# Attention into a mixture of experts on one core: batch 0's routing at earlier steps, casts dealt to other engines, weight loads placed otherwise

## The chip, the cores and the metric

One core of a Trainium2 chip runs the whole program. Times are device microseconds (us) of one execution. PE is TensorE, DVE is VectorE, ACT is ScalarE, POOL is GpSimd, and SP is the engine that only issues DMAs here.

## The reference, cut to what matters

There are three parts, one after the other. First comes attention over 2 batches of 8 heads with 768 rows and head size 64, in which a row sees only the keys of its own hash bucket. Its output, 1536 tokens of 512 numbers, goes through a layer of 8 experts, and that through a dense layer.

```
mask   = q_bucket[:, :, :, None] == k_bucket[:, :, None, :]
scores = np.where(mask, scale * q @ k.T, -1e9);  attn = softmax(scores);  x = attn @ v
expert_idx = argmax(x @ w_gate);  gate = softmax(x @ w_gate)[expert_idx]
disp[e, count[e]] = x[i]                     # tokens in order, up to capacity
out[i] = gate[i] * relu(disp[e] @ w1[e]) @ w2[e]
g = h * clip(h + 3, 0, 6) / 6  with  h = out @ w_in;   result = g @ w_out
```

To find a token's place, the kernel needs the expert of every token before it. This is the routing. It can be done for batch 0 once batch 0's heads are through, and for batch 1 only after the last head.

## The kernel before, in words

Products that need float32 precision are made from two f16 halves each: a high half (a cast) and a low half (the difference, scaled). So every weight, probability and activation is split into `h` and `l` tiles.

**Attention** is a loop over 96 steps `k`, six for each of 16 heads. In step `k` PE makes the scores of one tile of 128 keys (L442, L443), ACT takes the exponential into `pf` (L444), `high` casts it to `phi` (ACT L452, or DVE L454), `low` two steps later makes `plo` (L458, POOL or DVE), and four or five steps later `pv` multiplies both by v (L470 to L472). The row maxima of `mx` (PE L425, DVE L428) run eight steps ahead. All other work is put into the loop by the tables of `Q`: `at(k, f)` calls `f` at step `k`, and `spread(k, gen, d)` runs a generator piece by piece every `d` steps. Within an engine the instructions run in the order in which they are emitted.

In the last 12 steps, 84 to 95, `Q["hl"]` lists the steps (less 84) whose `high` is DVE's, the others being ACT's, and `Q["ll"]` those whose `low` is POOL's, the others being DVE's. In the middle of the loop nearly every `low` is POOL's.

`route(b, ...)` (L207) is the routing of one batch in 20 pieces: maximum (L212), difference `dl` (L215), rank `sc`, one-hot `oh`, counts, the PE product `psr`, positions, and at the end six one-hots `ohr` of 128x128 (L263). `weigh(b)` (L267) makes the gate weights in seven pieces, up to `rg` (L203).

**Between attention and the experts** lie, in order: the last `pv`; `scaled` and `columns` (L480 to L488) on DVE; six ACT copies into `xp` (L845); `store(7)` of these rows to `xd` in DRAM (SP, L512); batch 1's routing on DVE; the products `windows` into `psw`, from which the token numbers `ids` come (L1096); `gather(0)` (POOL, L970), which reads the first expert's tokens from `xd`; then `gates` (L1103), `scale_x` (L978), and `make_x` (PE transposes L989, ACT `xh` L992, DVE `xl` L993) for the two tiles of 112 tokens; then the first product of expert 0, `gemm1` (L1006). `heat` (L1083) adds products that nothing reads.

**Weights.** `load_w(e, i, q)` loads 512 KB into one of six `raw` buffers (SP, L143). `high_w` casts on ACT (L157), `low_w` makes the low halves on DVE (L163) for all that `high_w` has listed, and `split_w` does both for 512 columns. Before the change the four tiles of w1 of expert 0 are loaded in steps 78 to 81, w1's first half is split in steps 88.5 to 94.5, its second half around the gather, and the four tiles of w2 are loaded behind `store(7)`, for SP issues them as soon as that store is issued.

From the first `gemm1` on, experts and dense layer follow without a gap on PE; the output rows are written at the end.

Of the kernel before, what the change touches and what calls it, by code (L numbers as in the profile page):

```python
# [9 lines left out]
F32 = mybir.dt.float32  # L10
# [11 lines left out]
NH = B * H  # L22
BITS = 6
NC = S // P
# [39 lines left out]
def moe_attention_kernel(ctx, tc, qk, v, vt, pj, wg, w1, w2, win, wout, out, cap):  # L64
    nc = tc.nc
    pe, act, dve, pool, sp = nc.tensor, nc.scalar, nc.vector, nc.gpsimd, nc.sync
# [16 lines left out]
    def persist(shape, dt, name):  # L83
        return const.tile(shape, dt, tag=name, name=name)

    xd = dram.tile([NT + 1, DM], F32, tag="xd", name="xd")
    ident = persist([P, P], F32, "ident")
    ones = persist([P, P], F32, "ones")
    upper = persist([P, P], F16, "upper")
# [47 lines left out]
    wp1 = opened(wctx, "wp1", 2, side="right")  # L137
# [11 lines left out]
    late = []  # L149
# [7 lines left out]
        act.activation(wh[e, i][:, c : c + n], r, AF.Copy, scale=(S1, S2)[i // 2])  # L157
        late.append((e, i, c, n, r))

    def low_w():  # L160
        while late:
            e, i, c, n, r = late.pop(0)
            dve.scalar_tensor_tensor(  # L163
                out=wl[e, i][:, c : c + n], in0=r, scalar=(S1, S2)[i // 2], in1=wh[e, i][:, c : c + n],
                op0=ALU.mult, op1=ALU.subtract, accum_out=wlo[:, nlo[0] : nlo[0] + 1],
            )
            nlo[0] += 1

    def split_w(wp, e, i, q):
        high_w(wp, e, i, 512 * q, 512)  # L170
        low_w()
# [35 lines left out]
    def route(b, psum):  # L207

        n = NC
        l3 = lg[:, b]  # L210
        t1 = rtile([n], f"mx{b}")
        dve.tensor_reduce(out=t1, in_=l3, axis=AX.X, op=ALU.max)  # L212
        yield
        dl = dl_t[b] = rtile([n, E], f"dl{b}")
        dve.tensor_tensor(out=dl, in0=l3, in1=bc(t1, E), op=ALU.subtract)  # L215
        yield
        sc = rtile([n, E], f"sc{b}")
        dve.scalar_tensor_tensor(out=sc, in0=dl, scalar=0.0, in1=mid(rank8, n), op0=ALU.is_ge, op1=ALU.mult)
        yield
        dve.tensor_reduce(out=t1, in_=sc, axis=AX.X, op=ALU.max)  # L220
        yield
        o = oh[:, b]
        dve.tensor_tensor(out=o, in0=sc, in1=bc(t1, E), op=ALU.is_equal)
        yield
        with nc.allow_low_precision("counts up to 6"):
            dve.tensor_reduce(out=rs[:, b], in_=o.rearrange("p c e -> p e c"), axis=AX.X, op=ALU.add)
        yield
        ps = psum()
        k3 = ps[:, 0 : n * E].rearrange("p (c e) -> p c e", e=E)
        for c in range(n - 1):  # L230
            pe.matmul(k3[:, c + 1 :], ident16, mid(o[:, c], n - 1 - c), start=c == 0, stop=False, skip_group_check=True)
        for i in range(b):
            pe.matmul(k3, ones16, mid(rs[:, i], n), start=False, stop=False, skip_group_check=True)
        pe.matmul(k3, upper, mid(rs[:, b], n), start=False, stop=True, skip_group_check=True)
        yield
        dve.tensor_tensor(out=sc, in0=k3, in1=o, op=ALU.mult)
        yield
        dve.tensor_reduce(out=pos[:, b], in_=sc, axis=AX.X, op=ALU.add)
        yield
        ge = rtile([n, NW + 1], f"ge{b}")  # L240
        dve.tensor_tensor(out=ge, in0=bc(pos[:, b], NW + 1), in1=mid(edges, n), op=ALU.is_ge)
        yield
        dve.tensor_reduce(out=t1, in_=ge[:, :, 1:NW], axis=AX.X, op=ALU.add)
        dve.tensor_tensor(out=jo[:, b], in0=ge[:, :, 0:NW], in1=ge[:, :, 1 : NW + 1], op=ALU.subtract)
        yield
        place = rtile([n], f"pl{b}")
        dve.scalar_tensor_tensor(out=place, in0=t1, scalar=-float(GW), in1=pos[:, b], op0=ALU.mult, op1=ALU.add)
        jt = rtile([n, NW], f"jt{b}")
        dve.scalar_tensor_tensor(
            out=jt, in0=bc(tokid[:, b * n : (b + 1) * n], NW), scalar=1.0, in1=jo[:, b], op0=ALU.add, op1=ALU.mult  # L250
        )
        yield
        spots(rh[:, b], o, jt, pool if b else dve)
        yield
        for c in range(n):
            if not b:
                yield
            if b and c == n - 1:
                off = rtile([P], "off")
                act.activation(off, iota_r, AF.Square, bias=place[:, c : c + 1], scale=-1.0)  # L260
                act.activation(ohr[:, b, c], off, AF.Relu, bias=1.0, scale=-1.0)
                continue
            dve.tensor_scalar(  # L263
                out=ohr[:, b, c], in0=iota_r, scalar1=place[:, c : c + 1], scalar2=None, op0=ALU.is_equal
            )

    def weigh(b):  # L267

        n = NC
        ex = rtile([n, E], f"ex{b}")  # L270
        act.activation(ex, dl_t[b], AF.Exp, scale=isw[:, 0:1])
        yield
        se = rtile([n], f"se{b}")
        dve.tensor_reduce(out=se, in_=ex, axis=AX.X, op=ALU.add)
        yield
        dve.tensor_scalar(out=se, in0=se, scalar1=EPS, scalar2=None, op0=ALU.add)
        yield
        dve.reciprocal(out=gt[:, b], in_=se)
        yield

        jt = rtile([n, NW], f"jg{b}")
        dve.tensor_tensor(out=jt, in0=jo[:, b], in1=bc(gt[:, b], NW), op=ALU.mult)
        j2 = rtile([n, 2 * NW], f"j2{b}", F16)
        dve.tensor_copy(j2[:, :, 0:NW], jt)
        yield
        dve.tensor_tensor(out=jt, in0=jt, in1=j2[:, :, 0:NW], op=ALU.subtract)
        dve.tensor_scalar(out=j2[:, :, NW:], in0=jt, scalar1=LS, scalar2=None, op0=ALU.mult)
        yield
        spots(rg[:, b], oh[:, b], j2)
# [8 lines left out]
                )  # L298


    Q = {'v': (-3.25, -4.75, -1.75, -2.25), 'vg': (-4.5, -4.75), 'vgd': 1, 'pr': (-13.0, -12.75, -12.0, -12.5), 'prd': 0.6, 'b0': 7.75, 'b': 1.75, 'bd': 0.5, 'vm0': (8.0, 8.25, 10.75, 13.0), 'vm': (-0.5, 4.75, 7.0, 12.25), 'vs': 13.25, 'pa': 1.5, 'ev': 0.5, 'lvt': -5.0, 'v4': (2.0, 3.75, 4.0, 16.25), 'vg0': (1.85, -4.4, 7.75), 'p2': 3.5, 'lr': (0, 3, 1.5, 4.5), 'lv': 5.5, 'vsd': 0.75, 'ac': (0, 0, 2, 6, 7, 8, 9, 10), 'hd': (3, 5, 17), 'hn': (4, 4, 2, 2, 4, 3, 0, 0, 0), 'ap': (0,), 'h0': (7,), 'hl': (4,), 'l0': (), 'll': (1, 10), 'ht': (5, 9)}


    with ExitStack() as actx:
# [38 lines left out]
        def misc(name):  # L343
            return ps_x.tile([P, 512], F32, tag="x", name=name)
# [412 lines left out]
        def at(k, f, *args):  # L757
            later.setdefault(k, []).append((f, args))

        def spread(k, gen, d=1):  # L760


            def part(k):
                if next(gen, gen) is not gen:
                    at(k + d, part, k + d)

            at(k, part, k)
# [18 lines left out]
        for h in range(NH):  # L786
# [8 lines left out]
            elif h < NH - 1:  # L795
                at(k + Q["pa"], pair, h // 2)
                at(NC * h + Q["lvt"], load_vt, h // 2 + 1)
        spread(66, route(0, lambda: misc("psr0")), 1.5)
        spread(84, weigh(0))
        spread(89, any_unmatched())  # L800
        for i in range(4):
            at(NC * (NH - 3) + i, load_w, 0, i // 2, i % 2)
            at(STEPS - 7.5 + 2 * i, split_w, wp1, 0, 0, i)

        def due(k):
            for q in sorted(q for q in later if q <= k):
# [3 lines left out]
        for k in range(STEPS + LAG + 2):  # L810
# [17 lines left out]
                    pv(u)  # L828
            due(k)
        assert not later  # L830
        tally(NH // 2 - 1, pool, (0,))
        ru = nc.values_load(nflag[0:1, NH // 2 : NH // 2 + 1], min_val=0, max_val=NH * S)
        with tc.If(ru > 0):
# [11 lines left out]
            act.activation(xp_t[h // 2][:, c, DE : DE + D], sums[0][:, c, 0:D], AF.Copy, scale=sums[1][:, c])  # L845
        store(h // 2)
        rgen = route(1, lambda: misc("psr2"))
        for _ in range(8):
            next(rgen)
        heat(ps_t, "t", 2)  # L850


# [129 lines left out]
    def make_x(e, j):  # L982
        if j == 0:
            xs_t[e] = tuple(xp.tile([P, KD, W], F16, tag=n, name=f"{n}{e}") for n in ("xh", "xl"))
        xh, xl = xs_t[e]
        t = xg_t.pop((e, j))
        ps = ps_a.tile([P, KD, P], F32, tag="a", name=f"psa{e}{j}")
        for k in range(KD):
            pe.transpose(ps[:, k], t[:, k * P : (k + 1) * P], ident)  # L989
        c = slice(j * GW, (j + 1) * GW)  # L990
        ps = ps[:, :, 0:GW]
        act.activation(xh[:, :, c], ps, AF.Copy, scale=SX)  # L992
        dve.scalar_tensor_tensor(out=xl[:, :, c], in0=ps, scalar=SX, in1=xh[:, :, c], op0=ALU.mult, op1=ALU.subtract)  # L993
# [96 lines left out]
    windows(ps1, ohr, rh, range(B - 1))  # L1090
    wgen = weigh(1)
    next(wgen)
    windows(ps2, ohr, rg, range(B - 1))
    run(rgen)
    windows(ps1, ohr, rh, [B - 1])
# [8 lines left out]
    dve.scalar_tensor_tensor(  # L1104
        out=gates, in0=ps2[:, :, NW:], scalar=1.0 / LS, in1=gates, op0=ALU.mult, op1=ALU.add
    )
    split_w(wp1, 0, 1, 0)
    split_w(wp1, 0, 1, 1)
    for j in range(2):
        scale_x(0, j)  # L1110
    for j in range(2):
        make_x(0, j)
    for q in range(2, 4):
        split_w(wp1, 0, 1, q)
    for q in range(4):
        load_w(0, 2 + q // 2, q % 2)
    tgen = totals(lambda: ps_a.tile([P, KD * P], F32, tag="a", name="psc"))
    cgen = compact(lambda: ps_a.tile([P, KD * P], F32, tag="a", name="psi"))

# [354 lines left out]
```

## Time and profile before

| what | us |
|---|---|
| median of 3 runs (range) | 677.04 (676.58 to 677.83) |
| the profiled execution's own time | 675.88 |
| its span, first to last instruction | 674.1 |
| PE busy in it | 638.4 (95%) |
| DVE busy | 481.0 (71%) |
| ACT busy | 426.6 (63%) |
| POOL busy | 229.8 (34%) |

The mean granted clock of PE over the span is 0.981 of full speed. Read the shares by stage: attention lies in 0 to 238 us, the stretch between attention and experts in 238 to 255 us, the experts in 255 to 411 us, and the dense layer after that. In a chain of waits each line is the piece of work that the next line waited for, so the chain ends with the program. In a timeline the bracket behind an instruction is the time its engine stood idle before it, and who ended that.

### The profile page before, as it was taken

The page shows a single profiled execution, that of the slowest core. Times are in us where ns is not written, and L with a number is a line of the kernel's source. Part 1 is how long each engine was busy: PE and PEld are TensorE (multiplying, and loading weights), DVE is VectorE, ACT ScalarE, POOL GpSimd, SP SyncE. Part 2 cuts the span into 40 slices and gives each one's busy share as a digit, 9 for nine tenths or more (in the row PEclk, how much of TensorE's full clock was granted, in tenths as well). Part 3 has the DMA queues.
Part 4 walks back from the last instruction along what each step waited for, and adds up shares of the span by engine and source line. Part 5 has one row for each costly group of instructions (what it writes and reads, how often), then busy time and mean ns, then how long its engine had stood idle before and what let it go on. Part 6 is the DMA issues. An engine that isn't in the chain of part 4 may idle for free.

```text
span 674.1 us, 14367 instructions
## 1 busy us (share of the span) xinstructions
PE 638.4 (95%) x5518; PEld 479.7 (71%) x5518; DVE 481.0 (71%) x1038; ACT 426.6 (63%) x869; POOL 229.8 (34%) x199
## 2 busy tenths in 40 slices
PE   7899999999999769999999999999999999999894
PEld 2588889989899638999999997555555555555541
DVE  6768898898999957888888877888888452222320
ACT  3467778778787826776667765455445576555730
POOL 4339769769778233221077500000000021000011
PEclk9889999999999978999999999999999999999998
DMA  8584764764465065777677735443442011000011
GB/s 236 127 233 115 231 177 122 233 169 109 126 160 165 25 217 193 250 246 257 213 253 228 243 115 162 137 145 126 150 134 92 0 48 48 1 0 1 1 41 59
DMA packets 37840, 94.14 MB, mean 140 GB/s; under 512 B 7576, under 2 KB 13720, under 8 KB 37760
## 3 DMA queue, kind: packets, MB, share of 16 engines
q1 hardware_dynamic: 34672, 85.71, 42.7%
q0 software_dynamic: 2400, 7.36, 3.2%
q8 instruction: 46, 0.75, 0.4%
q14 instruction: 34, 0.28, 0.1%
q10 hardware_dynamic: 688, 0.03, 0.1%
HBM read 67.14 MB, written 6.29 MB: 109 GB/s over the span
## 4 chain that ended last, share of the span: by engine, by line
PE 75%; DVE 10%; DMA 6%; ACT 5%; issue 2%; SPq 0%; POOL 0%; POOLq 0%; ACTq 0%; DVEq 0%
PE psg L1249 16%; PE pso L1276 15%; PE psh L1006 11%; PE psy L1033 11%; PE psm L425 5%; PE pst L442 4%; PE pst L443 3%; DVE mx L428 2%; DMA out_dram<-os,inv 2%; PE psv L470 2%; PE psv L471 2%; PE psv L472 2%; PE psg L531 2%; DMA vr<-in_v_dram 1%; ACT junk L1203 1%
## 5 line engine op out<-in xcount | busy, mean ns | idle before, releaser
L458 POOL TENSOR_TENSOR plo<-pf,phi 128x768 f16<-128x768 f32 x86 | 147.1, 1736 | 60.4 <-ACT phi L452 24.9
L444 ACT ACTIVATE pf<-pst 128x384 f32<-128x384 f32 x192 | 83.5, 486 | 47.4 <-PE pst L443 45.7
L428 DVE TENSOR_REDUCE mx<-psm 128x1 f32<-128x384 f32 x192 | 96.3, 548 | 20.0 <-PE psm L425 19.7
L1291 POOL DMA_INDIRECT out_dram<-os,inv x12 | 12.1, 1008 | 270.8 <-DVE os L1283 244.5
L163 DVE SCALAR_TENSOR_TENSOR wl<-raw,wh 128x1024 f16<-128x1024 f32 (+1 forms) x68 | 82.7, 1218 | 6.3 <-ACT wh L157 5.2
L1249 PE MATMUL psg<-yTh,ch 128*128 128x512 f16 (+1 forms) x256 | 83.4, 326 | 3.2 <-DVE rl L1252 3.2
L1249 PE MATMUL psg<-yTl,ch 128*128 128x512 f16 (+1 forms) x256 | 83.4, 326 | 0.0
L1249 PE MATMUL psg<-yTh,cl 128*128 128x512 f16 (+1 forms) x256 | 83.4, 326 | 0.0
L1252 DVE SCALAR_TENSOR_TENSOR rl<-rl,psg 128x512 f32<-128x512 f32 x64 | 35.0, 551 | 64.4 <-ACT rl L1251 64.0
L442 PE MATMUL pst<-Y,K 128*128 128x384 f32 x192 | 75.2, 392 | 2.0 <-ACT pf L444 2.0
L1249 PEld LDWEIGHTS <-ch 128*128 128x128 f16 x512 | 50.0, 98 | 35.9
L452 ACT ACTIVATE phi<-pf 128x768 f16<-128x768 f32 x85 | 71.7, 844 | 1.9
L1276 PE MATMUL pso<-ch,gh 128*128 128x512 f16 x192 | 72.8, 379 | 0.0
L1276 PE MATMUL pso<-ch,gl 128*128 128x512 f16 x192 | 72.8, 379 | 0.0
L1276 PE MATMUL pso<-cl,gh 128*128 128x512 f16 x192 | 72.8, 379 | 0.0
L425 PE MATMUL psm<-K,X 76*128 76x384 f32 x192 | 66.8, 431 | 4.6 <-DVE mx L428 3.8
L157 ACT ACTIVATE wh<-raw 128x1024 f16<-128x1024 f32 (+1 forms) x68 | 67.6, 999 | 0.5 <-issue 0.4
L1276 PEld LDWEIGHTS <-gh 128*128 128x128 f16 x384 | 37.6, 98 | 42.3
L443 PE MATMUL pst<-X,K 77*128 77x384 f32 x192 | 66.5, 346 | 0.0
L1033 PE MATMUL psy<-hh,wl 128*128 128x224 f16 x256 | 66.3, 259 | 0.0
L1033 PE MATMUL psy<-hh,wh 128*128 128x224 f16 x256 | 66.3, 259 | 0.0
L1033 PE MATMUL psy<-hl,wh 128*128 128x224 f16 x256 | 66.3, 259 | 0.0
(231 smaller groups left out, 1495.2 us busy)
## 6 DMA issues: line engine op xcount, KB each, us to landing
raw<-in_w_dram SPq DMA_DIRECT2D x64, 512.0 KB
rc<-in_win_dram SPq DMA_DIRECT2D x16, 512.0 KB
rc<-in_wout_dram SPq DMA_DIRECT2D x16, 512.0 KB
r<-in_qk_dram SPq DMA_DIRECT2D x16, 384.0 KB
K<-hi SPq DMA_DIRECT2D x31, 192.0 KB
vr<-in_v_dram SPq DMA_DIRECT2D x4, 768.0 KB
vt<-in_vt_dram SPq DMA_DIRECT2D x8, 384.0 KB
Y<-hi SPq DMA_DIRECT2D x16, 192.0 KB
```

The lines of the kernel that those rows point to most:

```text
L163: dve.scalar_tensor_tensor(out=wl[e, i][:, c : c + n], in0=r, scalar=(S1, S2)[i // 2], in1=wh[e, i][:, c : c + n], op0=ALU.mult, op1=ALU.s ...
L425: pe.matmul(ps[:, :HS], st["X"][0:76, c::NC], st["K2"][0:76, n * HS : (n + 1) * HS], start=True, stop=True)
L428: dve.tensor_reduce(out=mm[:, c, n : n + 1], in_=ps[:, :HS], axis=AX.X, op=ALU.max)
L442: pe.matmul(ps[:, :HS], st["K1"][:, kc], st["Y"][:, qc], start=True, stop=False)
L443: pe.matmul(ps[:, :HS], st["K2"][0:77, kc], st["X"][0:77, qc], start=False, stop=True)
L444: act.activation(pf.rearrange("k (c n p) -> k c n p", c=NC, n=2)[:, :, n], ps[:, :HS].rearrange("k (p c) -> k c p", c=NC), AF.Exp, scale=0 ...
L452: act.activation(phi_t[k], pf_t[k], AF.Copy)
L458: eng.tensor_tensor(out=plo_t[k], in0=pf_t.pop(k), in1=phi_t[k], op=ALU.subtract)
L1006: pe.matmul(ps, l[:, c], r[:, k], start=n == 0, stop=n == 3 * KD - 1)
L1033: pe.matmul(ps, l, r, start=n == 0, stop=n == 3 * KF - 1)
L1249: pe.matmul(ps, l, x, start=n == 0, stop=n == 3 * KD - 1)
L1276: pe.matmul(po[blk][s], l, r, start=first and n == 0, stop=last and n == 2)
```

## The change

- Batch 0's `route` begins at step 57 instead of 66, and its `weigh` at step 75 instead of 84.
- Of the last 12 steps' `high`, DVE takes steps 88, 90, 92 and 94 instead of 88 alone. The `low` of step 94 goes from POOL to DVE.
- In the loop only two of the four splits of w1's first half are left whole (88.5 and 91), the third is cast at step 93; the remaining casts of `high_w` stand behind the loop and in batch 1's routing, and their `low_w` are put one by one into places in which DVE waits.
- w1's loads move from steps 78 to 81 to steps 81.5 to 84.5, the loads of w2's first half from behind `store(7)` to steps 88 and 89. The loads of w2's second half stand behind a DMA of one number, `held`, that reads the gathered tile `xg` after `scale_x`, so SP waits there.
- `make_x` of tile 0 is emitted ahead of `scale_x` of tile 1. Idle products: 5 before the gates and 6 (was 9) behind them, and new ones, 3 behind `make_x` of tile 0 and 2 behind that of tile 1.

```diff
+    held = dram.tile([1, 1], F32, tag="held", name="held")
...
-    def low_w():
-        while late:
+    def low_w(most=99):
+        for _ in range(min(most, len(late))):
...
-    Q = { ... 'hl': (4,), 'l0': (), 'll': (1, 10), 'ht': (5, 9)}
+    Q = { ... 'hl': (4, 6, 8, 10), 'l0': (), 'll': (1,), 'ht': (5, 6, 3, 2)}
...
-        spread(66, route(0, lambda: misc("psr0")), 1.5)
-        spread(84, weigh(0))
+        spread(57, route(0, lambda: misc("psr0")), 1.5)
+        spread(75, weigh(0))
         spread(89, any_unmatched())
         for i in range(4):
-            at(NC * (NH - 3) + i, load_w, 0, i // 2, i % 2)
-            at(STEPS - 7.5 + 2 * i, split_w, wp1, 0, 0, i)
+            at(STEPS - 14.5 + i, load_w, 0, i // 2, i % 2)
+        for i in range(2):
+            at(STEPS - 8 + i, load_w, 0, 2, i)
+            at(STEPS - 7.5 + 2.5 * i, split_w, wp1, 0, 0, i)
+        at(STEPS - 3, high_w, wp1, 0, 0, 1024, 512)
...
         assert not later
+        high_w(wp1, 0, 0, 1536, 512)
+        for q in range(2):
+            high_w(wp1, 0, 1, 512 * q, 512)
+        low_w(1)
         tally(NH // 2 - 1, pool, (0,))
...
         rgen = route(1, lambda: misc("psr2"))
-        for _ in range(8):
+        for _ in range(7):
             next(rgen)
+        low_w(1)
+        next(rgen)
         heat(ps_t, "t", 2)
...
     next(wgen)
+    high_w(wp1, 0, 1, 1024, 512)
     windows(ps2, ohr, rg, range(B - 1))
...
-    split_w(wp1, 0, 1, 0)
-    split_w(wp1, 0, 1, 1)
-    for j in range(2):
-        scale_x(0, j)
-    for j in range(2):
-        make_x(0, j)
-    for q in range(2, 4):
-        split_w(wp1, 0, 1, q)
-    for q in range(4):
-        load_w(0, 2 + q // 2, q % 2)
+    high_w(wp1, 0, 1, 1536, 512)
+    low_w(1)
+    scale_x(0, 0)
+    low_w(1)
+    make_x(0, 0)
+    heat(HT[2])
+    scale_x(0, 1)
+    make_x(0, 1)
+    heat(HT[3])
+    sp.dma_start(out=held, in_=xg_t[0, 1][0:1, 0:1])
+    for q in range(2):
+        load_w(0, 3, q)
```

## Rows read from the trace of the kernel before

**Rows 1.** The chain that ended last, whole run: start us, us, what.
```profile
247.42 5.70 DMA xg<-xd,ids
...
255.04 2.02 PE psh L1006 x12
...
257.09 9.00 PE psh L1006 x84
...
276.25 9.20 PE psh L1006 x96
```

**Rows 2.** DVE by line, 219 to 236 us: count, busy us, mean ns, idle before.
```profile
L458 DVE TENSOR_TENSOR plo<-pf,phi 128x768 f16<-128x768 f32 x8 | 7.6, 948 | 0.0
...
L263 DVE TENSOR_SCALAR ohr<-iota_r,pl 128x128 f16<-128x128 f16 x6 | 2.8, 473 | 0.0
...
L163 DVE SCALAR_TENSOR_TENSOR wl<-raw,wh 128x512 f16<-128x512 f32 x4 | 2.7, 682 | 0.1
...
L203 DVE TENSOR_TENSOR rg<-oh,j 128x384 f16<-128x384 f16 x1 | 0.6, 552 | 0.0
...
L454 DVE CAST phi<-pf 128x768 f16<-128x768 f32 x1 | 0.6, 551 | 0.0
```

**Rows 3.** DVE in order of time: start, us, line, operation, idle before and its releaser.
```profile
177.84 1.03 DVE L215 TENSOR_TENSOR dl<-lg,mx 128x48 f32<-128x48 f32 x1
...
233.60 1.63 DVE L263 TENSOR_SCALAR ohr<-iota_r,pl 128x128 f16<-128x128 f16 x1
...
238.13 0.22 DVE L480 TENSOR_SCALAR rd<-psv,sc 128x6 f32<-128x6 f32 x1 [1.09 <-PE psv L472]
...
239.41 0.21 DVE L215 TENSOR_TENSOR dl<-lg,mx 128x48 f32<-128x48 f32 x1
...
241.34 0.21 DVE L236 TENSOR_TENSOR sc<-psr,oh 128x48 f32<-128x48 f32 x1 [0.73 <-PE psr L234]
...
243.99 0.19 DVE L1096 CAST ids<-psw 128x32 int32<-128x32 f32 x1 [0.33 <-PE psw L295]
...
246.96 0.19 DVE L1104 SCALAR_TENSOR_TENSOR gates<-psg,gates 128x32 f32<-128x32 f32 x1
...
250.79 0.55 DVE L978 TENSOR_SCALAR xg<-xg,gates 128x512 f32<-128x512 f32 x1 [2.42 <-issue]
...
253.54 0.62 DVE L993 SCALAR_TENSOR_TENSOR xl<-psa,xh 128x448 f16<-128x448 f32 x1
```

**Rows 4.** ACT in order of time, same columns.
```profile
233.85 0.84 ACT L452 ACTIVATE phi<-pf 128x768 f16<-128x768 f32 x1
...
238.92 1.33 ACT L845 ACTIVATE xp<-psv,rd 128x64 f32<-128x64 f32 x6 [4.23 <-DVE xp L488]
```

**Rows 5.** POOL in order of time, same columns.
```profile
233.13 2.04 POOL L458 TENSOR_TENSOR plo<-pf,phi 128x768 f16<-128x768 f32 x1 [11.71 <-PE psv L472]
...
245.81 1.31 POOL L970 DMA_INDIRECT xg<-xd,ids  x1 [2.69 <-DMA raw<-in_w_dram]
```

**Rows 6.** The gathers' line L970, 16 of them: issue to landing.
```profile
DMA to landing us min/median/max: 3.9/5.2/7.2
```

**Rows 7.** SP's queue in order of time: store 6 and store 7 issued.
```profile
220.43 0.55 SPq L512 DMA_DIRECT2D xd<-xp  x1
...
240.28 0.54 SPq L512 DMA_DIRECT2D xd<-xp  x1
```

**Rows 8.** GB/s of 219 to 226 us in 40 slices (0.175 us each).
```profile
GB/s 0 0 0 0 0 0 0 17 1 0 0 0 0 0 0 196 331 295 316 307 304 313 182 3 0 0 0 0 0 0 0 0 0 0 0 0 0 0 0 0
```

**Rows 9.** PE by line, 238 to 255 us, columns as Rows 2.
```profile
L989 PE MATMUL psa<-ident,xg 128*128 128x128 f32 x8 | 1.3, 283 | 3.5 <-DVE xg L978 3.5
```

**Rows 10.** One microsecond: length, busy us (PE, PEld, DVE, ACT, POOL), PEclk, DMA share, GB/s.
```profile
255.00:256.00 1.00, 0.96 (x8) 0.85 (x8) 0.98 (x2) 1.00 (x3) 0.93 (x2) 0.73 0.00 0
```

**Rows 11.** Columns as Rows 10, from the row maxima of heads 7 and 11 to the next.
```profile
116.08:128.44 12.36, 12.05 (x152) 10.97 (x149) 10.93 (x28) 10.27 (x20) 7.89 (x8) 1.00 0.72 184
...
168.05:180.78 12.73, 12.29 (x150) 10.96 (x148) 11.75 (x31) 10.71 (x21) 7.98 (x7) 1.00 0.68 174
```

More of the change, by code (lines that the diff above doesn't have):

```diff
@@ L298, in windows @@
                 )
-    Q = {'v': (-3.25, -4.75, -1.75, -2.25), 'vg': (-4.5, -4.75), 'vgd': 1, 'pr': (-13.0, -12.75, -12.0, -12.5), 'prd': 0.6, 'b0': 7.75, 'b': 1.75, 'bd': 0.5, 'vm0': (8.0, 8.25, 10.75, 13.0), 'vm': (-0.5, 4.75, 7.0, 12.25), 'vs': 13.25, 'pa': 1.5, 'ev': 0.5, 'lvt': -5.0, 'v4': (2.0, 3.75, 4.0, 16.25), 'vg0': (1.85, -4.4, 7.75), 'p2': 3.5, 'lr': (0, 3, 1.5, 4.5), 'lv': 5.5, 'vsd': 0.75, 'ac': (0, 0, 2, 6, 7, 8, 9, 10), 'hd': (3, 5, 17), 'hn': (4, 4, 2, 2, 4, 3, 0, 0, 0), 'ap': (0,), 'h0': (7,), 'hl': (4,), 'l0': (), 'll': (1, 10), 'ht': (5, 9)}
+    Q = {'v': (-3.25, -4.75, -1.75, -2.25), 'vg': (-4.5, -4.75), 'vgd': 1, 'pr': (-13.0, -12.75, -12.0, -12.5), 'prd': 0.6, 'b0': 7.75, 'b': 1.75, 'bd': 0.5, 'vm0': (8.0, 8.25, 10.75, 13.0), 'vm': (-0.5, 4.75, 7.0, 12.25), 'vs': 13.25, 'pa': 1.5, 'ev': 0.5, 'lvt': -5.0, 'v4': (2.0, 3.75, 4.0, 16.25), 'vg0': (1.85, -4.4, 7.75), 'p2': 3.5, 'lr': (0, 3, 1.5, 4.5), 'lv': 5.5, 'vsd': 0.75, 'ac': (0, 0, 2, 6, 7, 8, 9, 10), 'hd': (3, 5, 17), 'hn': (4, 4, 2, 2, 4, 3, 0, 0, 0), 'ap': (0,), 'h0': (7,), 'hl': (4, 6, 8, 10), 'l0': (), 'll': (1,), 'ht': (5, 6, 3, 2)}
     with ExitStack() as actx:
@@ L985, in make_x @@
         xh, xl = xs_t[e]
-        t = xg_t.pop((e, j))
+        t = xg_t[e, j]
         ps = ps_a.tile([P, KD, P], F32, tag="a", name=f"psa{e}{j}")
```

## The prediction

> **What bounds the kernel now.** I read the chain of waits first, because it says where a change can reach the end. From 276 us on it is PE alone: 96 products of an expert take 9.20 us without a gap [rows 1], and the next expert begins where the last one ends. So whatever the change does up to the first product of expert 0 (255.04 us) moves the end one for one, and nothing behind it is touched unless weights come late. Second, DVE by line for 219 to 236 us, the last steps of attention [rows 2], and DVE, ACT and POOL in order of time [rows 3 to 5]. The reader is to see that DVE's last `low` ends at 237.04 (238.13 less the 1.09 of waiting), while ACT's last cast ended at 234.69 (233.85 + 0.84): DVE ends attention there. Third, the stretch 238 to 255 us: a serial chain of small DVE pieces, a store, a gather, and a first expert that starts at half clock.
>
> The sum is made against the profiled execution: 675.88 us, of which 674.1 is the span and 1.8 lies around it. The median of the three runs is 1.16 above it; I add that at the end.
>
> **Part 1, DVE in the last steps.** What leaves DVE behind 219 us: six `ohr` (2.8 us in all), two of the four `wl` (2 x 0.68 = 1.35), `rg` (0.55) [rows 2], and five small pieces of `weigh`, which I put at 0.2 each like the unhindered `dl` (0.21) of [rows 3]: together 5.7. What comes: three casts of 0.55 and one `plo` of 0.95 [rows 2], together 2.6. The net is 3.1 less. Neighbouring durations overlap at their ends, which favours the longer list, so I take 2.8, and 0.2 for PE, which no longer has several steps' products waiting when the last `low` comes: 3.0. ACT loses three casts of 0.84 [rows 4] and one weight cast, so it moves forward as far and DVE stays the last. Bounds: 0.5, if ACT or PE takes over, and 3.8. The two `wl` return at no cost: one stands behind the last `low`, where DVE waited 1.09, one in the wait for `psr` of 0.73 [rows 3], and each is 0.68 and an accumulator read. Without that cover they would cost 1.35. The three weight casts behind the loop stand on ACT, which was idle for 4.23 us ahead of the `xp` copies [rows 4].
>
> **Part 2, batch 0's routing earlier.** The pieces that leave the end go to steps 75 to 85, where POOL makes the `low`. There a DVE piece is not what it is alone: `dl` takes 1.03 us beside POOL against 0.21 without it, and the `ohr` of 233.60 takes 1.63 [rows 3], while POOL's `plo` runs from 233.13 to 235.17 [rows 5]; the other five take (2.8 - 1.63) / 5 = 0.24. So a piece can wait until POOL's instruction ends. POOL is busy 7.98 of 12.73 us in such a stretch [rows 11], so a piece meets it with a chance of 0.63 and waits half of 2.04: 0.64 us on average. Moved are six `ohr` at 0.24, `rg` and five small ones, 3.0 us, and they make some eight such meetings (pieces emitted together count once), 5.1 us: DVE gets 8.1 us more before step 87. What that does to the time is read from [rows 11]: between heads 11 and 12, where the maximum and `dl` of batch 0 lay, DVE was busy 0.82 longer than a period earlier, and the stretch was 0.37 longer, a share of 0.45. I take 0.45 x 8.1 = 3.6 us later. Bounds: nothing, as DVE has idle time there (0.98 us of 12.73), and all 8.1. The earlier pieces of `route` (steps 57 to 75 instead of 66 to 84) leave one busy stretch for another and cancel.
>
> The Trainium skill has a rule for this ("SBUF — State Buffer", section "Who interferes with whom"): a DVE instruction with two SBUF inputs, or one in a mode that uses both ports, and a POOL instruction that reads SBUF exclude each other, and the second one blocks fully. The trace agrees in `dl` and in `ohr`. By that rule alone every one of the moved pieces could wait out a whole POOL instruction, and attention would get longer by more than I take; that case is the slower rival below.
>
> **Part 3, store, gather, first tiles.** Store 6 was alone on the queues: issued at 220.43 [rows 7], its bytes move in slices 15 to 22 (counted from 0), until 223.0 [rows 8], 2.6 us after issue. Store 7 was issued at 240.28 with four loads of 512 KB straight behind it. The gather waited for 2.69 us until 245.81 for a DMA [rows 5], though the token numbers were there at 244.18 [rows 3]. The page names a weight load; the gather can only need the store. In the changed kernel nothing follows the store, so it lands near 243.0, and the token numbers are last: the gather starts at 244.25, 1.55 earlier. Its flight was 4.98 (245.81 to the scaling at 250.79 [rows 3]) beside the loads; without them I take 4.1, near the shortest of all gathers, 3.9 [rows 6]. So tile 0 is there at 248.35. The gates are ready at 247.15 [rows 3], the `wl` put behind them ends near 247.9, still under cover. From the landing of tile 1 (247.42 + 5.70 = 253.12) to the first product (255.04) it took 1.92 us [rows 1]; tile 0 needs that and 0.62 for its `xl` [rows 3], so DVE comes to tile 1 at 250.9, after its landing near 250.0, and the first product follows 1.92 later, at 252.8: 2.2 earlier. Bounds: 0.6, if the flight stays at 5.2 and only the start moves, less what the order on DVE costs, and 2.9.
>
> The added wait on SP holds back only the two loads of w2's second half and what follows them. They go out near 252 and are first needed by ACT half-way through the first `gemm1`, 4.6 us after its start (half of 9.20 [rows 1]), near 257.4; two loads of 512 KB at the 300 GB/s of the store [rows 8] take 3.5 us. I take nothing.
>
> **Part 4, the clock.** The first 96 products took 2.02 + 9.00 us against 9.20 later [rows 1]: 1.8 us lost, since the granted clock fell from 2.4 to 1.2 GHz in 255 to 256 (mean 0.73 [rows 10]), after PE had stood idle 3.5 us in two waits for `xg` [rows 9]. Earlier tiles and five idle products between them leave, by the times of part 3, about 1.3 us of idle. I take the whole 1.8; the other end is 0.
>
> **Sum:** +3.6 - 3.0 - 2.2 - 1.8 = -3.4 us, 672.5 for a profiled execution, 673.6 for the median.
>
> **Rivals.** (a) The waits for POOL are absorbed: PE and DVE have gaps, and the pieces fall into them. For it speaks POOL's 4.75 us idle in 12.73 [rows 11], against it that DVE is busy 11.75 of it. Then part 2 is 0: 670.0. (b) The clock still falls, as 1.3 us of idle remain: 675.4. (c) The tail is not DVE's: with shorter DVE work ACT's exponentials, or PE, set the pace, part 1 is worth 0.5: 676.1. Against it, ACT ended 2.35 us ahead of DVE and is relieved as well. (d) The weights behind the held DMA come some 2 us late, and ACT, which runs in order, keeps the first products waiting: 675.6. (e) Slower: the moved `ohr` and gate pieces wait for POOL and every wait reaches the end. At 1.39 for each of six `ohr` (1.63 - 0.24) and 0.82 for two others (1.03 - 0.21) that is 3.0 + 8.3 + 1.6 = 12.9 instead of 3.6: 682.9. It decides from 8.4 on, where it eats the 7.0 of the other parts and 1.35 more, that is, if all 8.1 pass and a little more. For it speaks that DVE is the busiest of the engines that could wait; against it the share of 0.45.
>
> **How the numbers follow.** About 0.2% (1.35 us) is what a measurement can tell from no change here: faster is under 675.69, slower over 678.39. Forecast 0.56, by itself 671.3 to 676.0 (0.51 faster, 0.05 same); (a) 0.13, faster; (b) 0.10 (0.06 faster, 0.04 same); (c) 0.07 (0.02, 0.05 same); (d) 0.05 (0.02, 0.03 same); (e) 0.09, slower. That is 0.74 faster, 0.17 same, 0.09 slower. The range 669.6 to 677.6 takes in (a) to (d) and leaves out (e) and the outer ends of the parts.
>
> **What would show it.** Part 1: DVE's wait before the first `rd` after the last `pv` shrinks to that of one step's products, and attention from the last row maximum to there takes about 3 us less. Part 2: the last row maximum (218.9 before) comes 3 to 4 us later, and `ohr` instructions of over 1 us stand in steps 78 to 85. Part 3: the gather begins within 0.2 us of the token numbers, and its flight is near 4. Part 4: the first 96 products take 9.2 to 9.4, with no granted clock under 1 after 249. The prediction fails if the last maximum moves by over 8 us or not at all, or if the gather still waits for a DMA.

## The result: slower by 1.2%, lost in the steps of attention that got batch 0's routing

The changed kernel takes 684.71 us (median; 683.97 to 685.02) against 676.81 of the kernel before in the same comparison: ratio 1.0116, 95% interval 1.0087 to 1.0144. Forecast were 673.6, with 677.6 as the upper end. The profiled execution of the changed kernel took 685.02 us, its span is 683.3 (before 675.88 and 674.1).

Where the time went can be read at five marks that both traces have: head 10's and head 15's last row maximum, the first `rd` behind the last `pv`, the first product of expert 0, and that of expert 1.

| stretch | before | after | difference |
|---|---|---|---|
| start to head 10's last maximum | 154.96 | 156.32 | +1.36 |
| heads 10 to 15 (steps 57 to 87) | 63.94 | 76.49 | +12.55 |
| last maximum to the last `rd` | 19.23 | 17.69 | -1.54 |
| `rd` to the first product of expert 0 | 16.91 | 14.77 | -2.14 |
| expert 0 | 21.21 | 19.77 | -1.44 |
| sum: start of expert 1 | 276.25 | 285.04 | +8.79 |

The rest of the 9.2 us of span, 0.4, lies in the output writes. The first line is not the change's: it arises before head 3's maximum (65.53 against 64.16), where both programs are the same, behind a stretch of half clock at 54 to 58 us. Two executions of one and the same kernel, `e1_old_steps` and `e11_old_steps_again` below, have head 3's maximum at 65.89 and at 64.14.

So three of the four parts brought something, and part 2 cost more than all of them. First the three stretches that hold 11.45 of its 12.55, in the kernel before (length; busy us of PE, PEld, DVE, ACT, POOL with counts; granted clock; DMA share; GB/s):

```profile
180.78:194.66 13.88, 13.61 (x177) 12.66 (x174) 13.21 (x29) 10.44 (x20) 13.04 (x8) 1.00 0.32 76
194.66:206.11 11.45, 11.07 (x137) 10.09 (x136) 10.32 (x22) 9.86 (x18) 7.93 (x8) 1.00 0.89 238
206.11:218.90 12.79, 12.79 (x163) 12.00 (x160) 11.90 (x30) 9.94 (x20) 10.40 (x7) 1.00 0.41 134
```

and the same steps in the changed kernel:

```profile
183.24:199.75 16.51, 14.39 (x166) 13.08 (x163) 14.94 (x31) 11.31 (x22) 14.64 (x9) 0.95 0.39 101
199.75:216.31 16.56, 12.98 (x141) 11.88 (x139) 15.87 (x30) 10.00 (x18) 10.22 (x8) 0.81 0.40 102
216.31:232.81 16.50, 16.50 (x162) 15.67 (x160) 11.91 (x29) 9.95 (x19) 6.81 (x5) 0.73 0.36 129
```

The middle row shows DVE busy for 15.87 of 16.56 us with one instruction fewer than in the row above it. The last row shows something else: there DVE is busy for no longer than before (11.91), and PE, at a mean granted clock of 0.73, is busy without a gap. DVE in order of time, the changed kernel:

```profile
188.41 1.62 DVE L242 TENSOR_TENSOR ge<-pos,edges 128x30 f32<-128x30 f32 x1
...
195.15 1.62 DVE L248 SCALAR_TENSOR_TENSOR pl<-mx,pos 128x6 f32<-128x6 f32 x1
...
204.15 1.29 DVE L277 TENSOR_SCALAR se<-se 128x6 f32<-128x6 f32 x1
...
209.34 1.01 DVE L283 TENSOR_TENSOR jg<-jo,gt 128x24 f32<-128x24 f32 x1
210.39 1.56 DVE L285 CAST j<-jg 128x24 f16<-128x24 f32 x1
211.86 1.70 DVE L264 TENSOR_SCALAR ohr<-iota_r,pl 128x128 f16<-128x128 f16 x1
```

In the kernel before, `jg` and its cast had no `low` of POOL beside them (DVE in order of time):

```profile
221.19 0.27 DVE L282 TENSOR_TENSOR jg<-jo,gt 128x24 f32<-128x24 f32 x1
221.49 0.18 DVE L284 CAST j<-jg 128x24 f16<-128x24 f32 x1
```

POOL in order of time, the changed kernel (the first row is three instructions of 1.6 each, and the second begins with the third of them):

```profile
208.66 4.84 POOL L459 TENSOR_TENSOR plo<-pf,phi 128x768 f16<-128x768 f32 x3 [1.63 <-PE pst L444]
211.86 3.23 POOL L459 TENSOR_TENSOR plo<-pf,phi 128x768 f16<-128x768 f32 x2
```

`jg` ends at 210.35, its cast at 211.95, `ohr` at 213.56: each at the end of one POOL instruction. 24 numbers per partition take 1.0 and 1.6 us instead of 0.27 and 0.18. I read it so: between two pieces that DVE issues back to back POOL starts its next `low`, and the second piece waits for all of it; `e6_pool_halves` below tests that. PE then waits for the row maxima behind this pile (PE in order of time, the same kernel):

```profile
214.07 0.70 PE L426 MATMUL psm<-K,X 76*128 76x384 f32 x1 [3.58 <-DVE mx L429]
```

and its granted clock falls while it stands (one microsecond each, columns as in Rows 10):

```profile
211.00:212.00 1.00, 0.00 (x0) 0.00 (x0) 1.00 (x2) 0.97 (x2) 1.00 (x2) 0.82 0.38 105
212.00:213.00 1.00, 0.00 (x0) 0.00 (x0) 1.00 (x1) 0.09 (x1) 1.00 (x1) 0.50 0.01 3
...
225.00:226.00 1.00, 1.00 (x16) 1.00 (x15) 0.42 (x2) 0.00 (x0) 1.00 (x1) 0.85 0.44 176
```

It is at 1.2 GHz from 211.7 to 225.3, and there PE is the engine without idle time, while DVE waits for its products. A shorter stretch of this kind lies at 198 to 201.

What answers to [rows 3] to [rows 5] behind attention, DVE in order of time and POOL in order of time:

```profile
250.50 0.22 DVE L481 TENSOR_SCALAR rd<-psv,sc 128x6 f32<-128x6 f32 x1 [0.34 <-PE psv L473]
...
256.14 0.19 DVE L1107 CAST ids<-psw 128x32 int32<-128x32 f32 x1 [0.33 <-PE psw L296]
...
261.04 0.48 DVE L988 TENSOR_SCALAR xg<-xg,gates 128x512 f32<-128x512 f32 x1 [1.11 <-issue]
```

```profile
257.30 1.08 POOL L980 DMA_INDIRECT xg<-xd,ids  x1 [2.02 <-DVE j L285]
```

The weight load that [rows 5] named is gone from the gather's wait, and tile 0 is scaled 3.74 us after the gather's issue instead of 4.98. The store that the gather reads from, SP's queue in order of time, and GB/s of 252 to 259 us in 40 slices (its last bytes move near 255.9):

```profile
252.64 0.56 SPq L513 DMA_DIRECT2D xd<-xp  x1
```

```profile
GB/s 0 0 0 0 0 0 0 0 94 0 70 310 328 322 316 322 310 179 23 20 23 20 3 0 0 0 0 0 0 0 0 0 0 0 0 0 0 0 0 0
```

What answers to [rows 1], from the chain that ended last, and to [rows 10]:

```profile
265.27 1.31 PE psh L1016 x12
...
285.04 9.20 PE psh L1016 x96
```

```profile
265.00:266.00 1.00, 0.80 (x9) 0.73 (x8) 0.75 (x2) 1.00 (x2) 0.65 (x1) 1.00 0.63 106
```

Expert 0 begins at full clock.

### The profile page after: what moved, and what is told of

Same layout as the page of the kernel before. It is cut to its first block, busy times and chain, and to the rows that moved or that the text cites. A ratio compares the mean times of both kernels' runs of the same rounds, so it can differ in the third digit from the quotient of the medians.

```text
span 683.3 us, 14368 instructions
## 1 busy us (share of the span) xinstructions
PE 644.5 (94%) x5520; PEld 485.1 (71%) x5520; DVE 488.0 (71%) x1042; ACT 424.9 (62%) x866; POOL 225.6 (33%) x198
## 4 chain that ended last, share of the span: by engine, by line
PE 53%; ACT 3%; DMA 3%; DVE 2%; issue 1%; POOL 0%; POOLq 0%; DVEq 0%
PE psg L1262 16%; PE pso L1289 15%; PE psy L1043 11%; PE psh L1016 10%; DMA out_dram<-os,inv 2%; ACT junk L1216 1%; PE psa L999 1%; ACT gh L1272 1%; DVE rl L1265 1%; DVE wl L164 0%; ACT rl L1264 0%; DMA xg<-xd,ids 0%; ACT xh L1002 0%; DVE hl L1020 0%; DVE xg L988 0%
## 5 line engine op out<-in xcount | busy, mean ns | idle before, releaser
L459 POOL TENSOR_TENSOR plo<-pf,phi 128x768 f16<-128x768 f32 x85 | 143.8, 1715 | 60.2 <-ACT phi L453 30.5
L426 PE MATMUL psm<-K,X 76*128 76x384 f32 x192 | 68.6, 437 | 11.9 <-DVE mx L429 10.3
L453 ACT ACTIVATE phi<-pf 128x768 f16<-128x768 f32 x82 | 69.2, 843 | 1.9
L426 PEld LDWEIGHTS psm<-K,X 76*128 76x128 f32 x192 | 53.8, 313 | 20.7 <-DVE mx L429 16.3
L471 PE MATMUL psv<-vh,phi 128*128 128x73 f16 x576 | 67.5, 202 | 0.0
L473 PE MATMUL psv<-vh,plo 128*128 128x73 f16 x576 | 66.8, 200 | 0.5 <-DVE plo L459 0.4
```

The source lines that it names most:

```text
L426: pe.matmul(ps[:, :HS], st["X"][0:76, c::NC], st["K2"][0:76, n * HS : (n + 1) * HS], start=True, stop=True)
L453: act.activation(phi_t[k], pf_t[k], AF.Copy)
L459: eng.tensor_tensor(out=plo_t[k], in0=pf_t.pop(k), in1=phi_t[k], op=ALU.subtract)
```

## The experiments

"Stretch" is the one from head 10's last row maximum to head 15's: 63.94 us before, 76.49 in the changed kernel. Stretches are from one trace each. Ratios are to the kernel before, taken beside it, with 95% intervals. Beside `e1_old_steps` to `e4_gather_alone` the kernel before took 680.82 us, 4 more than above, so their medians are to be read against that. Some traces hold a wait of the kind told under "not expected" in unchanged steps, worth 4.6 us in `e1_old_steps` and 5.7 in `e2_steps_alone`; so the stretch tells more than the median.

**The steps undone, and the steps alone.** `e1_old_steps` is the changed kernel with

```
-        spread(57, route(0, lambda: misc("psr0")), 1.5)
-        spread(75, weigh(0))
+        spread(66, route(0, lambda: misc("psr0")), 1.5)
+        spread(84, weigh(0))
```

> The changed kernel with batch 0's route and weigh back at steps 66 and 84, all else changed. Theory P (the moved pieces meet POOL's low instructions, DVE is held, PE waits for row maxima and its clock falls): the last row maximum, 232.8 us in the changed kernel, comes back to 219 to 221, no half clock in attention, and the time is 672 to 676. Rival Q (the routing's steps are harmless; the weight loads bunched at steps 81.5 to 84.5 and the casts given to DVE delay attention): the last maximum stays near 232 and the time at 683 to 686.

`e2_steps_alone` is the kernel before with the opposite edit and nothing else.

> The kernel before with only batch 0's route and weigh moved to steps 57 and 75. P: the last row maximum moves from 218.9 to about 231, the clock is at half in parts of 195 to 230, DVE's end of attention gets shorter by 2 to 4, and the time is 683 to 689, slower than before. Q: the last maximum within 1.5 us of before and the time 674 to 677.

Measured: ratio 0.9938 (0.9885 to 0.9991) for the first (679.08 us), 1.0184 (1.0080 to 1.0289) for the second (694.32). The last maxima, at 225.56 and 239.22, missed the expected times, as both traces lose over 6 us before head 10. The windows of the stretch, first of `e1_old_steps`, then of `e2_steps_alone`:

```profile
161.55:225.56 64.01, 62.59 (x770) 57.58 (x768) 58.34 (x137) 51.87 (x98) 52.29 (x35) 1.00 0.52 138
```

```profile
161.58:239.22 77.64, 71.13 (x772) 65.25 (x768) 66.51 (x149) 52.70 (x98) 51.77 (x35) 0.87 0.43 114
```

The steps alone bring the whole loss, and without them the moved loads and shared casts add nothing to the stretch. The rival with the loads and casts is out. The second kernel's tail from the last maximum to `rd` is 18.00, the first one's 19.00, before 19.23; 2 to 4 us less were expected of the second.

**One piece elsewhere.** `e3_onehots_on_act` is the changed kernel with batch 0's one-hots on ACT:

```
-            if b and c == n - 1:
+            if not b or c == n - 1:
```

> The changed kernel with the six one-hots ohr of batch 0 made on ACT (Square, then Relu, as batch 1's last one is), at the same steps. P: the three ohr that took 0.73, 1.70 and 1.37 us leave DVE, the other waits (sc, ge, place, the add, jg and its cast) stay; the pile of jg, cast and ohr at 209 to 213.5 gets shorter by its last 1.7, so part of the loss goes: 677 to 682. Q: no change, 683 to 686.

Measured: 1.0117 (1.0067 to 1.0167), 685.82 us, stretch 74.12. The expected time was missed: the three long `ohr` are gone, but the next pieces meet POOL in their place (the last two of `weigh` before `rg` take 0.76 and 1.56 us there, 0.73 and 0.18 in the changed kernel), and the clock falls at 211 all the same. Taking away these pieces was not enough while others made the same pile.

`e5_weigh_late` is the changed kernel with the gate weights alone at their old step:

```
-        spread(75, weigh(0))
+        spread(84, weigh(0))
```

> The changed kernel with weigh back at step 84 and route still at 57. The stretch from head 10's to head 15's last row maximum is 63.9 us in the kernel before and 76.5 in the changed one. Theory P (every moved piece waits out POOL's instruction, DVE falls behind, PE waits and its clock falls): the add, jg, its cast and the difference (1.29, 1.01, 1.56, 0.73 us) leave, so the pile at 209 to 213.5 is gone, PE's wait of 3.6 us shrinks and the clock holds at least after 212: stretch 68 to 72. If route's pieces alone do the harm (ge 1.62, place 1.62, ohr 1.70): 74 to 77.

Measured: 1.0033 (0.9998 to 1.0068), stretch 67.77 with DVE busy 61.25 and a mean clock of 0.97 (half clock at 192 to 195 alone). So `weigh` beside `route` makes 8.7 of the 12.55, and `route`'s own new steps 3.8.

**Shorter POOL instructions.** `e6_pool_halves` is the changed kernel with

```
+            x, n = pf_t.pop(k), S // 2 if eng is pool and k > 53 else S
+            for c in range(0, S, n):
+                eng.tensor_tensor(out=plo_t[k][:, c : c + n], in0=x[:, c : c + n], in1=phi_t[k][:, c : c + n], ...)
```

> The changed kernel with POOL's low from step 54 on made by two instructions of 384 columns instead of one of 768. If a DVE piece waits until the POOL instruction in flight ends and then has its turn, the waits halve to under 0.9 us each, PE's long wait goes and the clock holds: stretch of heads 10 to 15 at 65 to 70 us instead of 76.5, time near before or up to 4 us under it. If POOL's next instruction can go ahead of a waiting DVE piece, waits of 1.5 us and more stay and the stretch stays at 73 to 78.

Measured: 1.0088 (1.0055 to 1.0120), 682.82 us, and in its profile the stretch is 68.79. Window of the stretch, and two lines of DVE by line in it:

```profile
156.98:225.77 68.79, 63.84 (x770) 58.03 (x767) 62.75 (x148) 52.25 (x98) 57.65 (x65) 1.00 0.48 129
```

```profile
L219 DVE SCALAR_TENSOR_TENSOR sc<-dl,rank 128x48 f32<-128x48 f32 x1 | 0.9, 922 | 0.0
...
L285 DVE CAST j<-jg 128x24 f16<-128x24 f32 x1 | 0.8, 837 | 0.0
```

`sc` took 1.66 and this cast 1.56 in the changed kernel. Half the POOL instruction, about half the wait: in this stretch none of the routing's pieces takes as much as 0.9 us longer than alone, so they wait out POOL's instruction in flight. The clock stays full. The time was missed: the profiled execution took 678.14, but the median stayed 6 us over the kernel before; what the other executions lost was not profiled.

**The clock by itself.** `e8_idle_in_waits` is the changed kernel with products that nothing reads where PE waited:

```
+            if k in (75, 81):
+                hx = misc(f"hx{k}")
+                for _ in range(4 if k == 75 else 14):
+                    pe.matmul(hx, idle_sb[:, 0:P], idle_sb, start=True, stop=True)
```

> The changed kernel with idle products on PE ahead of the row maxima of steps 75 (4 of them) and 81 (14), where PE waited 0.84 and 3.58 us for DVE. If the fall of PE's clock is a good part of the loss: the granted clock stays full from 198 to 226, DVE's waits for POOL stay as they are, and the stretch of heads 10 to 15 falls from 76.5 to 69 to 72 us. If the clock is only a symptom and DVE's waits are all of it: the stretch stays at 75 to 78.

Measured: 1.0068 (1.0046 to 1.0089), stretch 71.39:

```profile
154.32:225.71 71.39, 67.99 (x789) 60.54 (x786) 65.65 (x149) 52.38 (x98) 52.83 (x35) 0.98 0.46 124
```

DVE's pieces wait as long as before (jg 1.01, its cast 1.56, `ohr` 1.70, as in the changed kernel), but the stretch has no half clock after 193.4, and 5.1 us come back: 76.49 - 71.39. That much of the loss, at least, goes with PE's clock; a half-clock stretch from 190.0 to 193.4 is still in the rest.

**The stretch behind attention by itself.** `e4_gather_alone` is the kernel before with parts 3 and 4 only (loads at steps 88 and 89 and behind the held DMA, tile 0 first, `'ht': (5, 6, 3, 2)`).

> The kernel before with only the stretch behind attention changed: w2's first half loaded at steps 88 and 89, the second half behind the held DMA, tile 0 made ahead of tile 1's scaling, idle products 5, 6, 3, 2. By parts 3 and 4 of the prediction the gather starts with the token numbers, the first product of expert 0 comes 2.2 us earlier after the last pv and runs at full clock: 672 to 674.5. If the flight or the clock does not follow: 675 to 677.

Measured: 0.9972 (0.9922 to 1.0022). Its profile has 34.63 us from the last `rd` (242.06) to expert 1 (276.69), the kernel before 38.12: 3.5 less, where parts 3 and 4 promised 4.0. Its first product comes 14.65 after `rd` instead of 16.91. The median (677.09 beside 680.82) does not show it clearly, for the interval includes 1.

**Versions that should do better.** `e7_old_steps_halves` is `e1_old_steps` with all of POOL's `low` in halves.

> The kernel of e1_old_steps (everything changed but batch 0's steps) with all of POOL's low in two instructions. If the waits for POOL cost time all through attention (vh, lo, dl, ge): 2 to 5 us less than e1, 668 to 671 against 676.8 of before in undisturbed runs, and fewer of the half-clock stretches that come and go between runs. If POOL's second instruction adds more than the shorter waits give: same as e1 or up to 3 us more.

Measured: 1.0314 (1.0231 to 1.0396), 698.86 us. This was expected wrongly, and the trace shows why. DVE in order of time, then POOL:

```profile
58.94 7.28 DVE L376 SCALAR_TENSOR_TENSOR lo<-r,hi 128x768 fp32r<-128x768 f32 x1
```

```profile
55.73 9.67 POOL L461 TENSOR_TENSOR plo<-pf,phi 128x384 f16<-128x384 f32 x11
```

A `lo` that takes 0.95 elsewhere in this trace is finished 0.8 us after POOL has run out of work. Three `vh` of 5.7 to 6.2 us stand in the same trace, each with a stretch of half clock behind it. `e1_old_steps` has one such wait with whole POOL instructions (`vh`, then POOL):

```profile
81.90 4.76 DVE L680 SCALAR_TENSOR_TENSOR vh<-vr,sc,vh 128x384 f16<-128x384 f32 x1
```

```profile
76.55 9.70 POOL L459 TENSOR_TENSOR plo<-pf,phi 128x768 f16<-128x768 f32 x6
```

`e9_vlow_on_pool` takes these `vh` off DVE:

```
+            if h > 3:
+                act.activation(r, r, AF.Copy, scale=s)
             yield
+            if h > 3:
+                pool.tensor_tensor(out=t[:, :, VA + o : VA + o + D], in0=r, in1=t[:, :, o : o + D], op=ALU.subtract)
```

> The kernel of e1_old_steps with the low half of v (vh, L680) of heads 4 to 15 made by POOL itself, after a scaled copy on ACT, instead of by DVE. In e1's profile one vh on DVE took 4.76 us, over three POOL instructions back to back, and the clock fell behind it (86 to 94 us); e2_steps_alone shows the same at 132.9. If such waits of DVE for POOL are what comes and goes between runs: no vh wait is left, no half clock in attention after 60 us, runs scatter less, and the median is 2 to 5 us under e1's. If ACT's extra 0.5 us per head or POOL's extra load costs more: same as e1 or 1 to 4 us slower.

Measured: 1.0049 (1.0025 to 1.0073), 679.78 us, slower than the same kernel without this edit beside it (`e11_old_steps_again`, 673.51). In its profile no `vh` waits, but another instruction does; DVE in order of time:

```profile
86.91 6.87 DVE L376 SCALAR_TENSOR_TENSOR lo<-r,hi 128x768 fp32r<-128x768 f32 x1
```

`e10_onehots_act_old` is `e1_old_steps` with the edit of `e3_onehots_on_act`.

> The kernel of e1_old_steps with batch 0's six one-hots on ACT instead of DVE, at the old steps 87 to 94.5, where POOL is almost idle. They take 1.4 us of DVE's time at the end of attention and would add 6 x 0.7 to ACT. If DVE alone ends attention: the time from the last row maximum to the last rd falls from 19.0 to 17.8. If ACT takes over: it stays at 19 or rises to 21.

Measured: 0.9966 (0.9945 to 0.9986); from the last maximum (220.37) to `rd` (238.86) 18.5 us instead of 19.0, between the two that were expected: a third of the 1.5 us that the one-hots took on DVE in `e11_old_steps_again`. ACT's busy time there rises from 13.87 to 16.96, so ACT probably takes over some of the path; that was not tested by itself.

> The kernel of e1_old_steps once more, beside e9 and e10 on one chip and in more rounds: the ratio to the kernel before was 0.9938 (0.9885 to 0.9991); expected again 0.992 to 0.997, with every run that shows a vh of over 3 us or a half clock in attention some 4 us slower.

`e11_old_steps_again` measured 0.9961 (0.9941 to 0.9981), 673.51 us. Its stretch has no such wait:

```profile
154.94:218.93 63.99, 62.59 (x770) 57.60 (x768) 58.32 (x137) 51.84 (x98) 52.28 (x35) 1.00 0.52 138
```

Up to head 15 it runs with the kernel before (218.93 and 218.90), and expert 1 begins at 272.21 instead of 276.25. This version beats both, the kernel before by 0.4%: the change without its new steps for batch 0.

## Why the prediction was wrong, by its own steps

Its own sign of failure came true: the last maximum moved by 13.9 us, from 218.90 to 232.81, and not by 3 to 4.

**Part 2 failed, in one step: the share of 0.45.** The working counted the moved pieces and their meetings with POOL and gave DVE 8.1 us more; measured are 8.46 (66.72 against 58.26 busy in the stretch). To go from there to the time, it took one interval [rows 11], in which 0.82 us more of DVE had come with 0.37 more of time. That interval holds only two pieces, and its 0.98 us of DVE idle time could take up part of them. I read the slack as a stock that is spent once, not as a share. What the runs show in place of 0.45 is a share near 1: 7.45 us of time for 7.39 of DVE in `e8_idle_in_waits`, 4.85 for 4.49 in `e6_pool_halves`, both without most or all of the half clock. No run spread the same pieces thinly, so that it is their crowding that makes the share 1 is argued, not shown. And the step stopped at DVE: PE waits behind it, and its clock falls. That is 5.1 us, which stand in no term of the sum, although the same fall behind the gather was part 4. 7.45 and 5.1 make the 12.55; the 7.45 alone would have stayed inside the part's bound of 8.1.

That 8.1 came so near to 8.46 is partly luck, for faults in the count cancel. Pieces emitted together were counted once, but POOL gets in between two of them, as `jg` and its cast show. Against that, three of the six `ohr` took 0.25, without a wait, and POOL's `low` takes 1.6 us in these steps, not the 2.04 of [rows 5].

**Rival (e)** had the path right, every wait reaches the end. Its 12.9 for this part, where 12.55 were measured, is luck: it charged all of it to DVE, 1.39 for each of six `ohr`, while DVE got 8.46 more, only three `ohr` were held up (0.73, 1.70 and 1.37 us), and 5.1 came from PE's clock, which (e) does not have. Its chance of 0.09 rested on the share, against the sentence on the Trainium skill that stood beside it ("SBUF — State Buffer", section "Who interferes with whom"): the second instruction blocks fully. The trace agrees with that at 211.95 and 213.56.

**Part 1** was mis-sized: 1.54 instead of 3.0. What the routing's pieces gave by leaving is 1.23 (`e2_steps_alone`), what the dealt casts gave by themselves 0.23 (`e1_old_steps`). DVE's busy time from the last maximum to `rd` fell from 17.78 to 16.21; with the `wl` of 0.69 that now lies in the wait before `rd` set aside, 2.3 us left DVE's path where 2.8 had been taken. And DVE waits 0.24, 0.40 and 0.16 us for PE and ACT in this stretch, which the 3.0 did not have. After the last `low` (ends at 249.55) PE takes 0.95 us, 0.14 less than before, near the 0.2 expected. Rival (c) was true in part.

**Part 3** came out at 2.14 for 2.2 by luck, for it has the gather's last wait wrong. It took the end of the store's bytes for its landing and had the token numbers come last. In eleven traces (all but those of the kernel before and `e2_steps_alone`, where weight loads overlap the store) the gather begins 1.39 to 1.44 us after the store's last bytes, and 0.29 to 1.25 us after the token numbers. In the changed kernel these are 1.40 and 0.97 us (257.30, after 255.9 and 256.33). Counted from the store's issue the delay varies more (3.98 in `e8_idle_in_waits`, 4.95 in `e6_pool_halves`). So the gather still waits for the store to land, though the profile names a piece of DVE. Measured from `rd` it starts 0.88 earlier, not 1.55; its flight makes up for it, 3.74 instead of 4.1. The order on DVE cost nothing of the 0.2 that was taken.

**Part 4** nearly held: 1.44 of 1.8. The first 96 products take 9.25 instead of 10.88 us, with no clock under 1 from 260 to the end of expert 0. Of these 1.63 us, 0.2 are lost again: at 276.61 PE has waited 0.36 us for the last `wl` of w2 (0.17 before). No cast on ACT waits for a load there, so the loads behind the held DMA cost nothing that the trace shows.

## What to carry to other kernels

A piece that is moved off a crowded end goes somewhere, and its price there is what runs beside it, not what it took before: look up on the trace how long the same form takes while the other user of the port is busy, and add these up against the idle time of the engine that waits, which is spent once. Then ask who waits behind that engine, and whether its clock survives the wait. An early interval with little in it gives no share for a later one with much in it.

## What the runs showed of the hardware that was not expected

A DVE instruction can wait for more than the POOL instruction in flight. With POOL's instructions back to back it waited 4.76 us over three of them (`e1_old_steps`) and 7.28 us over some seven half-size ones (`e7_old_steps_halves`), until POOL ran out of work. In `e11_old_steps_again`, the same program as `e1_old_steps`, the same `vh` took 1.52 us amid eight POOL instructions back to back. The Trainium skill ("SBUF — State Buffer", section "Who interferes with whom") says that the one that issues first has the ports for its whole instruction and the other blocks fully; here the measurement goes beyond it. Why the turn is given at one time and not at another was not settled.

PE's clock did not come back as soon as PE was busy again: in the changed kernel its records show no gap from 214.1 on, and the granted clock is full only from 225.3.

A gather can still wait for a store whose bytes have all moved: in eleven traces it began 1.39 to 1.44 us after the last of them, steadier than its distance from the token numbers or from the store's issue. What fills that time was not settled.
